# Identity columns in the s products, gate maxima moved by transposes, and five weight granules staged in idle buffers

## The chip, the cores and the metric

The kernel is one program on one core of a Trainium2 chip. The metric is the device time of one execution in microseconds (us). Before the change the median of three runs is 662.71 us (661.94 to 662.95).

## What is computed

A recurrent attention layer (an mLSTM: four batches, eight heads, 768 steps, head size 40) feeds two dense stages on 3072 tokens of 320 numbers:

```python
m_new = max(f_gate[t] + m, i_gate[t])
C = exp(f_gate[t] + m - m_new) * C + exp(i_gate[t] - m_new) * outer(v[t], k[t])
n = exp(f_gate[t] + m - m_new) * n + exp(i_gate[t] - m_new) * k[t]
y[t] = sigmoid(o_gate[t]) * (C @ q[t]) / max(abs(n . q[t]), 1)
x = y.reshape(3072, 320)
h = (x @ w1) * (x @ w2) @ w3 @ w_out          # first stage, d_ff 1024
out = max(x2 @ a1, x2 @ a2, x2 @ a3) @ a_out  # second stage on x2 = h, d_ff 768
```

## The kernel before

**The recurrence in chunks.** Each batch is cut into nine chunks of L = 87 steps (the last has 72), so there are 36 units (`NU`). Unit q = 9b + c is worked on in a visit on TensorE (PE): `visit(v)` computes the s products of unit v (line 839, eight small fp32 products of k and q, one per head) and then the output products of unit v - 1 (line 848). Four heads have their 40 rows at partitions 0 to 39 and four at 64 to 103, and the loop alternates between the two. Each s product loads 87 columns (k) as weights and moves 87 columns (q) past them (72 in the last chunk). An fp32 product stands in the trace as two records, each with its own weight load, so one visit shows sixteen.

The s products are multiplied by decay factors `dd` on VectorE (DVE, line 873) into rows 0 to 86 of a tile `pk`. Rows 87 to 126 of `pk` belong to the state carried over from earlier chunks: there `scaled` (line 806, DVE or GpSimd (POOL)) multiplies q itself, transposed on the host and loaded as the last 696 columns of the tile `kv` (line 706), by `dd`. The output products contract all 127 rows (R = 127) at once. Chunk 0 of each batch has no state, so there is no `scaled` and R is 87. For the first nine units `dd` is made by PE (lines 757 and 758, from `hl`, `one`) and an exponential on ScalarE (ACT, line 761); for the others it is read back from `d_na` in HBM.

**The gates.** At the start, scans on DVE (lines 574 to 612) form the running gate maxima in `gft`. The ones of batch 0 have to come to rows 64 to 72 and 96 to 104 of `hl`: three DMAs write them to `d_na` (line 619), one reads them back (line 650), and ACT and DVE split them in two fp32r parts (lines 651 and 652).

**The weights.** Dense weights arrive as 64-bit numbers in granules of 128 x 512 (512 KB) or 128 x 256, and are turned to fp32 by two ACT or DVE steps (lines 1172, 1178, 1181) and one DVE step (line 1189). Granules rotate through seven buffers at the start: four of the pool `sx`, three of `stg`. `fold(ft)` multiplies w3 by w_out (line 1236, 16 fp32 records for each ft, 128 in all) and leaves it in `wb`; the first two folds run before the first visit, six more between the first visits. From then on the first dense stage (`a_step` and `b_step`, lines 970 to 975, 985 and 1082 to 1086) and the second (`c_step`, `d_step`, lines 970 to 975 and 1102) run, with one visit riding in a dense step now and then.

**Warm-up matmuls.** 22 matmuls of 128 x 512 on zeros (line 541) run at the start: 16 at once, six that wait for the first w_out granule.

**The order.** A planner (`Plan.run`) sorts all operations: each has an engine, a cost in ns, a rank in `PRIO` (lower goes first among those that are ready), and for some a choice of engine in `PICK`. Each engine then runs its operations strictly in the planned order. DMAs are all issued from the queue of SyncE (SP), in order; a DMA whose buffer isn't free holds up those behind it. Tiles share buffers in rotation by tag (`kv` 3, `raw` 2, `raw0` 3, `sx`, `stg`, and in PSUM `wk` 3, `aq` 1).

Of the kernel before, what the change touches and what calls it, by code (L numbers as in the profile page):

```python
# [17 lines left out]
L = 87  # L18
R = L + D
# [32 lines left out]
OC = 4 * L  # L52
BUF = dict(x=3, y=3, ph=2, ev=3, raw=2, kv=3, dd=3, pk=2)
# [12 lines left out]
    "11100111101000000100000110110011111101101111000111010011000110011110110011001110001111001011111110110000110010"  # L66
    "00001011101000111101100110011001101110001010010110011101001010110010111001101100101001110001001000001011111011"
    "10100110000001001110000011011110000100011011010111000100110110100000010000000000100100101000010100111101100110"
    "01000100010000101100001100010011010100110011110001011100000110011001110010111000000"
)  # L70
PRIO = (
# [95 lines left out]
)  # L167
WARM = 11500
USTEPS = (
    (0, 1, 3, 5, 8, 11, 14, 18, 22, 26), (0, 2, 4, 6, 8, 11, 14, 17, 20, 23, 26), (0, 2, 4, 6, 8, 9, 11, 12, 14, 15)  # L170
)
# [1295 lines left out]
```

## Time and profile before

| | us |
|---|---|
| median of three runs | 662.71 (661.94 to 662.95) |
| the profiled execution | 664.29 |
| its span, first to last instruction | 662.6 |
| TensorE busy within it | 648.7 (98%) |
| VectorE, ScalarE, GpSimd busy | 343.7, 296.1, 216.2 |
| HBM read, written | 71.18 MB, 4.03 MB |

The span is what the profile shows; the 1.7 us around it (664.29 less 662.6) aren't in the trace. Busy times of PE are made of records whose ends are modelled and overlap, so the distance between starts tells more of PE's pace than the length of a record. The granted clock of PE is given as a share of 2.4 GHz: 1.00 is that level, 0.50 is 1.2 GHz.

### The profile page before, as it was taken

How to read it: one execution, taken by the hardware profiler on the slowest of the kernel's cores; microseconds unless marked ns; L12 is line 12 of the kernel's file. 1: busy time of each engine (PE TensorE's matmuls, PEld its weight loads, DVE VectorE, ACT ScalarE, POOL GpSimd, SP SyncE). 2: the span in 40 equal slices, each digit the busy share in tenths (PEclk: the TensorE clock that was granted, in tenths of full speed). 3: DMA queues.
4: the chain of work that ended last, by engine and by line, in shares of the span. 5: the costliest groups of instructions: out<-in, count | busy, mean ns of one | idle time of the engine just before them, and what ended most of it. 6: DMA issues, size and time to landing. Idle time of an engine off the chain costs nothing.

```text
span 662.6 us, 14153 instructions
## 1 busy us (share of the span) xinstructions
PE 648.7 (98%) x5903; PEld 574.8 (87%) x5903; DVE 343.7 (52%) x623; ACT 296.1 (45%) x578; POOL 216.2 (33%) x235
## 2 busy tenths in 40 slices
PE   6899999999999999999999999999999999999997
PEld 5676899899999999999999988788788888888897
DVE  5688998877943663554543445464632321322222
ACT  7867986676622363453432343553331122322031
POOL 4052454566413234343244433562300013010030
PEclk9899999999999999999999999999999999999999
DMA  8989973545421453423122343342000010000011
GB/s 288 384 324 368 317 221 125 195 155 171 138 86 56 129 165 124 128 87 95 58 75 85 108 145 119 109 149 65 1 1 1 0 41 1 0 1 0 1 41 40
DMA packets 25489, 76.12 MB, mean 115 GB/s; under 512 B 3145, under 2 KB 6217, under 8 KB 25426
## 3 DMA queue, kind: packets, MB, share of 16 engines
q1 hardware_dynamic: 25426, 75.23, 33.8%
q8 instruction: 46, 0.75, 0.5%
q14 instruction: 17, 0.14, 0.1%
HBM read 71.18 MB, written 4.03 MB: 114 GB/s over the span
## 4 chain that ended last, share of the span: by engine, by line
PE 89%; DMA 3%; DVE 3%; ACT 3%; issue 1%; SPq 0%; ACTq 0%; DVEq 0%
PE wk L970 14%; PE wk L971 13%; PE wk L972 13%; PE wk L973 7%; PE acs L1102 6%; PE wk L975 5%; PE wk L1236 4%; PE aq L848 3%; PE acs L1082 3%; PE acs L1084 3%; PE acs L1086 3%; PE aq L839 3%; PE ac L1102 3%; PE ac L1082 2%; PE ac L1086 2%; PE wk L985 2%
## 5 line engine op out<-in xcount | busy, mean ns | idle before, releaser
L1049 DVE TENSOR_TENSOR misc<-misc,wk 128x384 f32<-128x384 f32 (+2 forms) x87 | 51.3, 594 | 130.5 <-PE wk L975 96.7
L997 ACT CAST hp<-misc 128x384 fp32r<-128x384 f32 (+2 forms) x101 | 55.0, 547 | 141.0 <-DVE misc L1049 53.1
L1001 POOL TENSOR_TENSOR hp<-misc,hp 128x384 fp32r<-128x384 f32 (+1 forms) x40 | 46.2, 1155 | 118.2 <-ACT hp L997 109.0
L970 PE MATMUL wk<-xx,wch 128*128 128x384 f32 (+1 forms) x216 | 77.3, 358 | 0.4 <-DVE misc L1049 0.4
L971 PE MATMUL wk<-xx,wcl 128*128 128x384 f32 (+1 forms) x216 | 76.5, 354 | 0.0
L972 PE MATMUL wk<-xx,wch 128*128 128x384 f32 (+1 forms) x216 | 76.5, 354 | 0.0
L1019 DVE TENSOR_TENSOR misc<-misc,wk 128x384 f32<-128x384 f32 (+1 forms) x56 | 33.8, 607 | 77.7 <-ACT misc L1017 53.2
L970 PE MATMUL wk<-xx,wah 128*128 128x384 f32 (+1 forms) x192 | 69.7, 363 | 1.1 <-DVE misc L1019 0.8
L971 PE MATMUL wk<-xx,wal 128*128 128x384 f32 (+1 forms) x192 | 68.1, 354 | 0.0
L972 PE MATMUL wk<-xx,wah 128*128 128x384 f32 (+1 forms) x192 | 68.0, 354 | 0.0
L1017 ACT COPY misc<-wk 128x384 f32<-128x384 f32 (+1 forms) x56 | 29.3, 522 | 54.8 <-PE wk L975 27.5
L1102 PE MATMUL acs<-wd,hp 128*128 128x320 f32 x234 | 52.7, 310 | 0.1
L1001 POOL TENSOR_TENSOR xx<-misc,hp 128x512 fp32r<-128x512 f32 (+1 forms) x15 | 18.2, 1215 | 95.5 <-ACT hp L997 91.3
L1046 ACT COPY misc<-wk 128x384 f32<-128x384 f32 (+1 forms) x42 | 22.1, 526 | 60.7 <-PE wk L975 46.2
L970 PEld LDWEIGHTS wk<-xx,wch 128*128 128x128 f32 x216 | 40.6, 188 | 3.7 <-DVE misc L1049 0.7
L972 PEld LDWEIGHTS wk<-xx,wch 128*128 128x128 f32 x216 | 40.5, 188 | 3.0
L971 PEld LDWEIGHTS wk<-xx,wcl 128*128 128x128 f32 x216 | 40.6, 188 | 2.8
L1236 PE MATMUL wk<-wof,w 128*128 128x320 f32 x128 | 38.4, 452 | 3.8 <-DVE wof L1189 2.3
L1102 PEld LDWEIGHTS acs<-wd,hp 128*128 128x128 f32 x234 | 40.0, 188 | 1.4 <-ACT misc L1145 0.3
L970 PEld LDWEIGHTS wk<-xx,wah 128*128 128x128 f32 x192 | 36.1, 188 | 4.6 <-DVE misc L1019 1.1
L972 PEld LDWEIGHTS wk<-xx,wah 128*128 128x128 f32 x192 | 36.1, 188 | 2.7
L973 PE MATMUL wk<-xx,wcr 128*128 128x384 f32 (+1 forms) x108 | 38.2, 354 | 0.0
(206 smaller groups left out, 1525.6 us busy)
## 6 DMA issues: line engine op xcount, KB each, us to landing
kv<-in_kv SPq DMA_DIRECT2D x32, 672.0 KB, 4.3
raw<-in_qk SPq DMA_DIRECT2D x36, 348.0 KB, 4.0
dd<-d_na SPq DMA_DIRECT2D x24, 348.0 KB, 3.8
sx<-in_w3t SPq DMA_DIRECT2D x9, 512.0 KB, 6.5
stg<-in_wc SPq DMA_DIRECT2D x9, 512.0 KB, 3.6
out<-misc SPq DMA_DIRECT2D x24, 160.0 KB, 1.9
stg<-in_w3t SPq DMA_DIRECT2D x6, 512.0 KB, 8.6
sx<-in_wa SPq DMA_DIRECT2D x6, 512.0 KB, 8.4
```

The source lines that it names most:

```text
L970: PE.matmul(p, lhsT=h_[:, kt], rhs=xh[:, kt], start=kt == 0, stop=False)
L971: PE.matmul(p, lhsT=l_[:, kt], rhs=xh[:, kt], start=False, stop=False)
L972: PE.matmul(p, lhsT=h_[:, kt], rhs=xl[:, kt], start=False, stop=False)
L973: PE.matmul(p, lhsT=r_, rhs=xh[:, 2], start=False, stop=False)
L975: PE.matmul(p, lhsT=r_, rhs=xl[:, 2], start=False, stop=True)
L997: P.op("A", act(n), lambda sl=sl: A.copy(out=T("ph", key)[:, sl], in_=T(*src)[:, sl]), r=[src + part], w=[("ph", key) + part])
L1001: e.tensor_tensor(out=T("pl", key)[:, sl], in0=T(*src)[:, sl], in1=T("ph", key)[:, sl].bitcast(F32), op=ALU.subtract)
L1019: P.op("V", dve(n), lambda: V.tensor_tensor(out=T(*sa), in0=T(*sa), in1=T(*ps[1]), op=ALU.mult), r=[ps[1]], w=[sa])
L1049: P.op("V", dve(sl.stop - sl.start), lambda sl=sl: V.tensor_tensor(out=T(*sc)[:, sl], in0=T(*sc)[:, sl], in1=T(*ps)[:, sl], op=ALU.max), r ...
L1082: PE.matmul(a, lhsT=w[:, o:o + 128], rhs=h_, start=st, stop=False)
L1102: PE.matmul(T(f"ac{m}", (k, 1)), lhsT=src[:, m * 128:m * 128 + 128], rhs=w[:, o:o + DM], start=first_, stop=last_,)
L1236: PE.matmul(T(*ps), lhsT=T(*w3)[:, i * 128:i * 128 + 128], rhs=wof[:, gt * 320:gt * 320 + 320], start=gt == 0, stop=gt == 7,)
```

## The change

- `raw` gets 40 identity columns behind k for each head (line 789: 214 columns a head in place of 174), from the host. The s products of chunks 1 to 8 load 127 columns as weights in place of 87, so that q itself comes out in PSUM rows 87 to 126 beside the scores. Line 873 then writes all 127 rows of `pk`, and `scaled` is gone. `kv` loses its 696 columns of q; it is 648 columns wide, or 968 where it brings the output gate (all units but the first five).
- The gate maxima of batch 0 go by PE: three transposes into PSUM, a copy to SBUF (`gt`), eight transposes into PSUM (`rp`), from where lines 651 and 652 read. The four DMAs of lines 619 and 650 are gone. `rp` takes the PSUM buffer `aq`, which the first visit uses next.
- Five early granules get other homes: three of w_out the three `kv` buffers, the two 256-column ones of w3 the two `raw` buffers, which unit 8 is the first to use. They no longer count in the rotation through `sx` and `stg`.
- Warm-up matmuls: 13 at once and 3 that wait for `git`, placed ahead of the new transposes, in place of 16 and 6.
- `PICK` and `PRIO` are new throughout, and the planner's constant for the slow clock (`WARM`) goes from 11500 to 8000. The planner's cost of the s products (775 ns) stays.

```diff
+RW = 4 * (2 * L + D)
 PICK = (
...
 PRIO = (
...
-WARM = 11500
+WARM = 8000
...
-        (big, "kv", BUF["kv"], 648 + 8 * L), (big, "raw", BUF["raw"], 8 * L),
+        (big, "kv", BUF["kv"], 1024), (big, "raw", BUF["raw"], RW),
...
-    for n, dep in ((16, ()), (6, (("wo", 0, 0),))):
+    for n, dep in ((13, ()), (3, (("g", "git"),))):
...
-    for i in range(3):
-        dma(100, lambda i=i: SP.dma_start(
-            out=d_na[0, 3 * i:3 * i + 3].rearrange("c h t -> h c t"), in_=c3(T("g", "gft"))[32 * i:32 * i + 8]
-        ), r=[("g", "gft")], w=[("dna", 0, i)])
+    warm(1)
+    new(("pt", 1), [128, 3, LP], F32, "ac0")
+    new(("rp", 0), [128, 2, 512], F32, "aq")
+
+    def f():
+        for c in range(3):
+            PE.transpose(T("pt", 1)[0:L, c, 0:L], c3(T("g", "gft"))[0:L, c], cs[0:L, 0:L])
+
+    P.op("P", 250, f, cols=200, r=[("g", "gft"), ("cs", 0)], w=[("pt", 1)])
+    P.op(("V", "A"), (dve(216), act(216, True)), (
+        lambda: V.tensor_copy(T("gt", 0)[:, :, 0:72], T("pt", 1)[0:L, :, 0:72]),
...
+    def f():
+        for h in range(8):
+            PE.transpose(T("rp", 0)[0:NCH, h // 4, h % 4 * LE:h % 4 * LE + L],
+                         T("gt", 0).rearrange("p c x -> p (c x)")[:, h:8 * 32 + h + 1:32], cs[0:L, 0:L])
+
+    P.op("P", 500, f, cols=400, r=[("gt", 0), ("cs", 0)], w=[("rp", 0)])
...
-    dma(150, lambda: SP.dma_start(out=raw_v, in_=d_na[0, :, :, 0:L]), r=[("dna", 0)], w=[("rv", 0)])
...
-        m = 648 + 8 * L if c else 648 + DM if b else 648
+        m = 648 + DM if (b, c) >= (0, SIGN) else 648
...
-        dma(950, lambda: SP.dma_start(out=T("raw", q).rearrange("p a b -> p (a b)"), in_=qk[b, c, :, 0:8 * L]), w=[("raw", q)])
+        dma(1165, lambda: SP.dma_start(out=T("raw", q).rearrange("p a b -> p (a b)"), in_=qk[b, c, :, 0:RW]), w=[("raw", q)])
...
-        if c:
-
-            def scaled(e):
-                qq = T("kv", q)[:, 648:648 + 8 * L].rearrange("p (h t) -> p h t", t=L)
-                e.tensor_tensor(out=T("pk", q)[64:R, :, 0:n], in0=qq[64:R, :, 0:n],
-                                in1=T("dd", q)[64:R, :, 0:n], op=ALU.mult)
-
-            P.op(("G", "V"), (1600, dve(8 * n)), (lambda: scaled(G), lambda: scaled(V)), r=[("kv", q, "x"), ("kv", q, "g"), ("dd", q)],
-                 w=[("pk", q, 1)], port=1)
...
-                        PE.matmul(s_of(v)[:L, g, h], lhsT=k[:, L:2 * L], rhs=k[:, 0:n], start=True, stop=True)
+                        PE.matmul(s_of(v)[:ub(v)[3], g, h], lhsT=k[:, L:L + ub(v)[3]], rhs=k[:, 0:n], start=True, stop=True)
...
-                out=by_g(T("pk", v)[:L, :, 0:n]), in0=s_of(v)[:L], in1=by_g(T("dd", v)[:L, :, 0:n]), op=ALU.mult
+                out=by_g(T("pk", v)[:rv, :, 0:n]), in0=s_of(v)[:rv], in1=by_g(T("dd", v)[:rv, :, 0:n]), op=ALU.mult
...
-        ng[0] += 1
-        p = "sx" if not switch and i % (STG + EX) < EX else "stg"
-        key = new((p, i), [128, 512, 2], I32, p)
+        ng[0] += not home
+        p = home or ("sx" if not switch and i % (STG + EX) < EX else "stg")
+        key = new(("gr", len(made)) if home else (p, i), [128, 256 if home == "raw" else 512, 2], I32, p)
...
-                granule(wo1[:, i * 512:i * 512 + 512], (("wo", 0, i), lambda i=i: wof[:, i * 512:i * 512 + 512]))
-            warm(1)
+                granule(wo1[:, i * 512:i * 512 + 512], (("wo", 0, i), lambda i=i: wof[:, i * 512:i * 512 + 512]),
+                        "kv" if i < 3 else None)
...
-                        (w3 + part, lambda w3=w3, o=o, n=n: T(*w3)[:, o:o + n]))
+                        (w3 + part, lambda w3=w3, o=o, n=n: T(*w3)[:, o:o + n]), "raw" if n < 512 else None)
```

## Rows read from the trace of the kernel before

**Rows 1.** The page: busy time by engine, and the chain that ended last.

```profile
PE 648.7 (98%) x5903; PEld 574.8 (87%) x5903; DVE 343.7 (52%) x623; ACT 296.1 (45%) x578; POOL 216.2 (33%) x235
PE 89%; DMA 3%; DVE 3%; ACT 3%; issue 1%; SPq 0%; ACTq 0%; DVEq 0%
```

**Rows 2.** Stretches: length, busy us and count by engine, clock, DMA share, GB/s.

```profile
0.00:12.00 12.00, 8.64 (x31) 6.76 (x31) 6.82 (x18) 8.93 (x15) 4.72 (x21) 1.00 0.83 287
12.00:17.00 5.00, 2.68 (x11) 1.58 (x10) 3.47 (x6) 3.65 (x7) 2.57 (x3) 1.00 0.95 291
17.00:21.00 4.00, 3.75 (x8) 2.50 (x9) 2.96 (x6) 1.82 (x4) 0.00 (x0) 0.58 1.00 397
21.00:26.00 5.00, 5.00 (x28) 3.37 (x28) 2.17 (x5) 4.53 (x8) 0.00 (x0) 1.00 0.99 335
...
55.00:72.00 17.00, 15.87 (x247) 12.12 (x234) 13.96 (x31) 13.65 (x30) 5.41 (x7) 1.00 1.00 377
72.00:200.00 128.00, 126.23 (x1289) 121.05 (x1288) 102.02 (x167) 87.70 (x175) 63.19 (x59) 1.00 0.51 164
200.00:662.00 462.00, 458.76 (x3916) 406.56 (x3914) 188.35 (x348) 155.30 (x303) 129.59 (x137) 1.00 0.21 65
```

**Rows 3.** PE's timeline at the start: start, us, work [idle before it, who ended it].

```profile
11.11 1.15 PE L659 MATMUL ac<-cs,misc 32*127 32x32 f32 x9 [1.29 <-ACT sx L1172]
12.56 2.42 PE L1236 MATMUL wk<-wof,w 128*128 128x320 f32 x8 [0.30 <-DVE w L1189]
17.25 8.42 PE L1236 MATMUL wk<-wof,w 128*128 128x320 f32 x24 [2.27 <-DVE wof L1189]
...
28.67 4.58 PE L1236 MATMUL wk<-wof,w 128*128 128x320 f32 x16 [1.05 <-ACT dd L761]
...
66.24 0.43 PE L757 MATMUL wk<-hl,hl 128*128 128x352 f32 x1 [1.13 <-ACT dd L761]
```

**Rows 4.** Pieces of the chain that ended last: start, us, what.

```profile
8.59 6.06 DMA sx<-in_w3t
...
17.25 4.12 PE wk L1236 x8
...
33.57 2.15 PE wk L1236 x8
```

**Rows 5.** Two riding visits in PE's timeline, with 87 and with 72 moving columns.

```profile
211.56 0.78 PE L839 MATMUL aq<-raw 40*87 40x87 f32 x16
212.27 0.81 PE L848 MATMUL aq<-kv,pk 127*32 127x41 f32 x64
...
230.37 0.77 PE L839 MATMUL aq<-raw 40*87 40x72 f32 x16
```

**Rows 6.** By source line: durations in ns, least, median and most, by form.

```profile
L839 PEld LDWEIGHTS aq<-raw x16: 152/154/154, 211.4 to 212.0; 40*87 40x87 f32 x16
L839 PE MATMUL aq<-raw x16: 235/237/238, 211.6 to 212.1; 40*87 40x87 f32 x16
...
L659 PEld LDWEIGHTS ac<-cs,misc x9: 180/186/186, 11.1 to 12.0; 32*127 32x127 f32 x9
L659 PE MATMUL ac<-cs,misc x9: 262/270/270, 11.1 to 12.0; 32*127 32x32 f32 x9
```

**Rows 7.** The same view for the two multiplications into `pk`.

```profile
L806 DVE TENSOR_TENSOR pk<-kv,dd x18: 757/881/2189, 40.3 to 448.3; 63x696 f32<-63x696 f32 x16, 63x576 f32<-63x576 f32 x2
...
L873 DVE TENSOR_TENSOR pk<-aq,dd x33: 755/878/880, 31.5 to 471.4; 87x696 f32<-87x696 f32 x29, 87x576 f32<-87x576 f32 x4
```

**Rows 8.** DVE's timeline around the first products and the gate maxima.

```profile
7.88 0.68 DVE L1189 SCALAR_TENSOR_TENSOR wof<-sx 128x512 int32<-128x512 int32 x1
...
24.79 0.88 DVE L652 TENSOR_TENSOR hl<-misc,hl 9x696 fp32r<-9x696 f32 x1 [0.87 <-ACT hl L651]
```

**Rows 9.** What SP waited for (us, times, longest), and DMA issues, 0 to 80 us.

```profile
SPq L650 <- DMA d_na<-misc: 2.8, 2, 2.6
...
kv<-in_kv SPq DMA_DIRECT2D x8, 672.0 KB, 8.1
```

More of the change, by code (lines that the diff above doesn't have):

```diff
@@ L65 @@
 PICK = (
[L66 to L69, printed above, removed]
+    "10110101111111000000111011101101010110000111100001110000100110101010010111111101111111111001000011110010110000"
+    "10101001101111110111001110110100100110001100010010000100001110010010000001011010010100110011011001111011001111"
+    "01001010000000011011110000110001000010111001100110111011110110101000110011110001001011010001101100101011111101"
+    "1010011001100110110010010000100101110111010010110000"
 )
 PRIO = (
[95 rows of a table removed]
[93 rows of a table added]
 )
-WARM = 11500
+WARM = 8000
 USTEPS = (
@@ L414, in mlstm_moe_kernel @@
         *((big, t, BUF[t], 8 * L) for t in ("dd",)), (big, "pk", BUF["pk"], 8 * R),
-        (big, "kv", BUF["kv"], 648 + 8 * L), (big, "raw", BUF["raw"], 8 * L),
-        (early, "sx", 3, 1024), (tmp, "sx", EX - 3, 1024), (tmp, "w3", L_BUFS, 512), (tmp, "raw0", RAW0, 8 * L),
+        (big, "kv", BUF["kv"], 1024), (big, "raw", BUF["raw"], RW),
+        (early, "sx", 3, 1024), (tmp, "sx", EX - 3, 1024), (tmp, "w3", L_BUFS, 512), (tmp, "raw0", RAW0, RW),
         (psum, "wk", 3, 512), (psum, "aq", 1, 1024),
@@ L524, in mlstm_moe_kernel @@
         o += n
-    made["rv", 0] = misc[:, o:o + 8 * L]
+    made["gt", 0] = misc[0:L, o:o + 3 * LP].rearrange("p (c x) -> p c x", x=LP)
     for tag, (x, y) in where.items():
-        if x < o + 8 * L and o < y:
-            over[tag].append(("rv", 0))
+        if x < o + 3 * LP and o < y:
+            over[tag].append(("gt", 0))
     def c3(t):
@@ L553, in f @@
         pick(cs[:, L:L + 1], cs[:, L:L + 1], -1, L - 1, [[0, 1]], ALU.is_ge, 1.0)
-        e = cs[:, L + 1:L + 1 + NCH]
+        e = cs[:, L + 1:L + 1 + NCH].rearrange("p (i c) -> p i c", c=3)
         for o in (64, 96):
-            pick(e, e, 1, -o, [[-1, NCH]], ALU.not_equal, -1.0)
+            pick(e, e, 1, -o, [[-1, 3], [-3, 3]], ALU.not_equal, -1.0)
     P.op("G", 1200, f, w=[("cs", 0)])
@@ L617, in mlstm_moe_kernel @@
     ), r=[("mp", 0, 0), ("mp", 0, 1)], w=[("g", "aug", 0)])
-    for i in range(3):
-        dma(100, lambda i=i: SP.dma_start(
-            out=d_na[0, 3 * i:3 * i + 3].rearrange("c h t -> h c t"), in_=c3(T("g", "gft"))[32 * i:32 * i + 8]
-        ), r=[("g", "gft")], w=[("dna", 0, i)])
+    warm(1)
[7 more added lines that the diff above has]
+        lambda: V.tensor_copy(T("gt", 0)[:, :, 0:72], T("pt", 1)[0:L, :, 0:72]),
+        lambda: A.copy(out=T("gt", 0)[:, :, 0:72], in_=T("pt", 1)[0:L, :, 0:72]),
+    ), r=[("pt", 1)], w=[("gt", 0)])
+    def f():
[3 more added lines that the diff above has]
+    P.op("P", 500, f, cols=400, r=[("gt", 0), ("cs", 0)], w=[("rp", 0)])
     P.op("G", 400, lambda: G.memset(T("hl", 1)[64:128].bitcast(F32), 0.0), w=[("hl", 1, 2), ("hl", 1, 3)])
@@ L648, in mlstm_moe_kernel, with by4 @@
     P.op("V", dve(NCH * 128), f, r=[("g", "aug"), ("hl", 0, 0)], w=[("hl", 0, 1)])
-    hi, raw_v = T("hl", 1)[64:64 + NCH, :, 0:L], T("rv", 0)[64:64 + NCH].rearrange("p (a b) -> p a b", b=L)
-    dma(150, lambda: SP.dma_start(out=raw_v, in_=d_na[0, :, :, 0:L]), r=[("dna", 0)], w=[("rv", 0)])
-    P.op("A", act(8 * L), lambda: A.copy(out=hi, in_=raw_v), r=[("rv", 0)], w=[("hl", 1, 2)])
-    P.op("V", dve(8 * L), lambda: V.tensor_tensor(
-        out=T("hl", 1)[96:96 + NCH, :, 0:L], in0=raw_v, in1=hi.bitcast(F32), op=ALU.subtract
-    ), r=[("rv", 0), ("hl", 1, 2)], w=[("hl", 1, 3)])
+    def by4(o):
+        return T("hl", 1)[o:o + NCH, :, 0:L].rearrange("p (g h) t -> p g h t", g=2)
+    raw_v = T("rp", 0)[0:NCH, :, 0:4 * LE].rearrange("p g (h t) -> p g h t", t=LE)[:, :, :, 0:L]
+    P.op("A", act(8 * L, True), lambda: A.copy(out=by4(64), in_=raw_v), r=[("rp", 0)], w=[("hl", 1, 2)])
+    P.op("V", dve(8 * L), lambda: V.tensor_tensor(out=by4(96), in0=raw_v, in1=by4(64).bitcast(F32), op=ALU.subtract),
+         r=[("rp", 0), ("hl", 1, 2)], w=[("hl", 1, 3)])
     new(("pt", 0), [128, NCH, 32], F32, "ac2")
@@ L663, in mlstm_moe_kernel @@
     sig = []
-    dma(1700, lambda: SP.dma_start(out=sg0.rearrange("p c d -> p (c d)"), in_=og),
+    dma(2050, lambda: SP.dma_start(out=sg0.rearrange("p c d -> p (c d)"), in_=og),
         w=[("sg", (0, c)) for c in range(SIGN)])
@@ L703, in load @@
         b, c, n, r = ub(q)
-        new(("kv", q), [128, 648 + 8 * L], F32, "kv")
-        m = 648 + 8 * L if c else 648 + DM if b else 648
-        dma(1.36 * m, lambda: SP.dma_start(out=T("kv", q)[:, 0:m], in_=kv[b, c, :, 0:m]), w=[("kv", q, x) for x in "kgx"])
+        new(("kv", q), [128, 648 + DM], F32, "kv")
+        m = 648 + DM if (b, c) >= (0, SIGN) else 648
+        dma(1.36 * m, lambda: SP.dma_start(out=T("kv", q)[:, 0:m], in_=kv[b, c, :, 0:m]), w=[("kv", q, x) for x in "kg"])
     def gates(b, c):
@@ L787, in prepare @@
         b, c, n, r = ub(q)
-        new(("raw", q), [128, 4, 2 * L], F32, "raw0" if q < NQ else "raw")
-        dma(950, lambda: SP.dma_start(out=T("raw", q).rearrange("p a b -> p (a b)"), in_=qk[b, c, :, 0:8 * L]), w=[("raw", q)])
+        new(("raw", q), [128, 4, 2 * L + D], F32, "raw0" if q < NQ else "raw")
+        dma(1165, lambda: SP.dma_start(out=T("raw", q).rearrange("p a b -> p (a b)"), in_=qk[b, c, :, 0:RW]), w=[("raw", q)])
         if (b, c) >= (0, SIGN):
@@ L871, in visit @@
         if v < NU:
-            n = GL[v % NCH]
+            n, rv = ub(v)[2:]
             P.op("V", dve(8 * n), lambda: V.tensor_tensor(
-                out=by_g(T("pk", v)[:L, :, 0:n]), in0=s_of(v)[:L], in1=by_g(T("dd", v)[:L, :, 0:n]), op=ALU.mult
+                out=by_g(T("pk", v)[:rv, :, 0:n]), in0=s_of(v)[:rv], in1=by_g(T("dd", v)[:rv, :, 0:n]), op=ALU.mult
             ), r=[*(t + ("s",) for t in toks), ("dd", v)], w=[("pk", v, 1)])
@@ L1152, in mlstm_moe_kernel, with granule @@
     ng = [0]
-    def granule(src, dst=None):
+    def granule(src, dst=None, home=None):
         n = src.shape[1]
         i = ng[0]
-        ng[0] += 1
-        p = "sx" if not switch and i % (STG + EX) < EX else "stg"
-        key = new((p, i), [128, 512, 2], I32, p)
+        ng[0] += not home
+        p = home or ("sx" if not switch and i % (STG + EX) < EX else "stg")
+        key = new(("gr", len(made)) if home else (p, i), [128, 256 if home == "raw" else 512, 2], I32, p)
         def tl():
@@ L1403, in _lay @@
     qk = pad(qk).reshape(B, 2, D, 2, 4, NCH, L).transpose(0, 5, 1, 2, 4, 3, 6)
-    rows = np.zeros((B, NCH, 128, 704), f)
-    rows[:, :, 0:D, 0:8 * L] = qk.reshape(B, NCH, 2, D, 8 * L)[:, :, 0]
-    rows[:, :, 64:64 + D, 0:8 * L] = qk.reshape(B, NCH, 2, D, 8 * L)[:, :, 1]
-    kvw = np.zeros((B, NCH, 128, 648 + 8 * L), f)
-    kvw[:, :, L:R, 648:] = qk[:, :, :, :, :, 0].transpose(0, 1, 3, 2, 4, 5).reshape(B, NCH, D, 8 * L)
+    one = np.broadcast_to(np.eye(D, dtype=f)[:, None], (B, NCH, 2, D, 4, D))
+    qk = np.concatenate([qk.reshape(B, NCH, 2, D, 4, 2 * L), one], -1).reshape(B, NCH, 2, D, RW)
+    rows = np.zeros((B, NCH, 128, 864), f)
+    rows[:, :, 0:D, 0:RW] = qk[:, :, 0]
+    rows[:, :, 64:64 + D, 0:RW] = qk[:, :, 1]
+    kvw = np.zeros((B, NCH, 128, 648 + DM), f)
     kvt = np.zeros((B, NCH, 128, H, 81), f)
```

188 rows, old and new, of the table PRIO are left out of this document.

## Prediction

> **What bounds the kernel now.** I read the page first: TensorE (PE) is busy for 648.7 of the span's 662.6 us, and 89% of the chain that ended last is PE [rows 1]. Then the table of stretches, to see where that holds [rows 2]. From 72 to 200 us PE is idle for 128.00 - 126.23 = 1.77 us, from 200 to 662 us for 462.00 - 458.76 = 3.24 us, in which the last evacuation lies too. From 72 us on the time is therefore the sum of PE's work, and DVE, POOL and DMA (busy shares in the same rows) have room. A microsecond more of work on PE there is a microsecond more of time; a microsecond less on another engine is nothing. Before 72 us it is different: PE has holes, ACT is busy for 8.93 + 3.65 + 1.82 + 4.53 = 18.9 of the first 26 us, and the DMA share is 0.83 to 1.00 [rows 2]. So the change has to be priced twice: in PE's work from 72 us on, and in the holes before.
>
> **The s products, on PE.** This is the term with the largest price. One visit's sixteen records run from 211.56 to 212.34 us (0.78 us); less the last record's own 0.237 us that is 0.543 us from first start to last start [rows 5, 6]. The two halves of the array (partitions 0 to 39, and 64 up) work side by side, so these are 8 pairs and 7 steps: 0.0776 us a step. What sets the step? With 72 moving columns in place of 87 the sixteen records take 0.77 us, not a sixth less [rows 5]. It isn't the moving columns, then; what both visits have in common is 87 weight columns. A second row shows the same from the other side: the nine transposes at 11.11 us move only 32 columns but load 127, and their step is (1.15 - 0.270) / 8 = 0.110 us at the full clock [rows 2, 3, 6]. 0.110 / 0.0776 = 1.42, and 127 / 87 = 1.46. The loads themselves take 154 ns for 87 columns and 186 ns for 127 [rows 6]: 32 ns more, as the steps do. So with the 40 identity columns I expect a step of 0.110 us: 0.0324 us more, 8 steps a visit, 0.26 us. Chunks 1 to 8 of four batches are 32 visits: 32 x 0.26 = +8.3 us. The low end is 7 steps in the 27 visits after the first folds, 27 x 7 x 0.0324 = +6.1 us, if the first load hides behind the matmul ahead of it and the five early visits fall into holes; the high end is +8.7 us, a load of 186 ns also ending later at the first step of each visit. I take +8.2. The output products read the same `pk` and keep their cost.
>
> The Trainium skill (TensorE: Matmul & The Clock Gate, Step-by-step: what each phase is for) says that throughput is purely N cycles, N being the moving columns. By that the extra weight columns would cost nothing. The trace doesn't bear it out for these small products: 0.77 against 0.78 us.
>
> **What leaves DVE, POOL and SP.** `scaled` goes: 18 instructions of 0.88 us on DVE and 14 on POOL [rows 7]. Line 873 now writes 127 rows, but its time is that of 696 elements a row, 878 ns on 87 rows just as line 806 takes 881 on 63 [rows 7], so it costs the same. This lies beside PE: from 72 us on PE idles 1.77 us up to 200 us for all reasons together [rows 2]. I take 0, bounds -1 and +1. The DMAs shrink: `kv` from 672 to 324 KB for chunks 1 to 4 of batch 0 and to 484 KB elsewhere, `raw` from 348 to 428 KB. Of the eight wide `kv` loads issued in the first 80 us [rows 9] that is about 2.1 MB less, of ten `raw` loads 0.8 MB more. At 340 GB/s the difference is some 4 us of DMA time, but it is worth something only where PE waits for data.
>
> **The start.** Four pieces are lost by PE once it has work: a hole of 2.27 us at 17.25; the eight products after it at the half clock (granted 0.58 on average in that stretch, hence 1.2 GHz for most of it), 4.12 us where eight take 2.15 later, 1.97 lost; a hole of 1.05 us at 28.67 and one of 1.13 us at 66.24 [rows 2 to 4]. Sum 6.4 us. The first hole ends with a w3 granule whose DMA was issued only at 8.59 us, because its `sx` buffer was being read by line 1189 until 7.88 + 0.68 = 8.56 us, and landed 6.06 us later [rows 4, 8]. With five granules in other buffers that DMA can be issued right behind the first ones; the 2.7 MB ahead of it (four granules of 512 KB, two of 256, the gates) at the 350 or so GB/s of these stretches would then have it in SBUF near 11 or 12 us instead of 14.65. The wait of SP for the `d_na` round trip (2.6 us, with w3 granules queued behind it) goes too [rows 9], and `hl`, which was ready only at 25.67 us, can be ready before 17. What is late next is ACT, 18.9 of 26 us busy: the same conversions have to fit in less. So I take the first hole and the half clock as gained (4.2 us) and of the two later holes, which wait for an exponential on ACT, about a third (0.8): -5.0 us. Bounds: 0, if PE still starts its dense run at 17.25; and -8.6, namely all 6.4 and 2.2 us more by doing the first eight products (2.42 us) ahead of 12.56 [rows 3].
>
> **What is added to PE and to the queues.** Eleven transposes at no more than the 0.110 us above are 1.2 us; they and the three later warm-up matmuls can lie in PE's idle time before 12.56 (1.29 us before the nine transposes) [rows 3]: between 0 and +1.2, I take +0.5. PE is strictly in order, so whatever stands behind them waits for `gft`, that is for the gate scans. The first s products now wait for lines 651 and 652, which read `rp` in the buffer `aq`; at some 0.9 us each [rows 8] behind the transposes they end well ahead of 20 us, so nothing. The homes in `kv` and `raw` cost nothing: w_out is out of them before the first `kv` load is wanted, and `raw` isn't used until unit 8.
>
> **The sum** is 8.2 - 5.0 + 0.5 = +3.7 us on the profiled execution's 664.29, 668.0. That execution stands 1.6 us above the median of 662.71, so for the median I give 666.4 us.
>
> **Rivals.** (A) The longer loads are hidden: the step stays at 0.0776 because the load of one half runs behind the matmul of the other. Then only the start counts: -5.0 + 0.5 = -4.5, 658.2 us. The equal times at 72 and 87 moving columns and the 0.110 us of the transposes speak against it; that those transposes all use the same rows of the array and the s products alternate speaks for it. The Trainium skill's rule of the moving columns would come out here. Chance 0.10.
> (B) The start gains enough to pay for the loads. The place is PE's holes in the first 30 us (and the one at 66.24), and it decides from a gain of 8.7 us on: all four pieces and the first products moved ahead of 12.56, practically the bound above. Then 8.2 - 8.6 + 0.5, about 662.8 us, not slower. For it: the w3 data can be there some 3 us sooner. Against: ACT's 18.9 busy us. Chance 0.12.
> (C) The change doesn't do at the start what it says: PE waits at 17.25 for something else (ACT, or the clock falls to 1.2 GHz after the shorter warm-up and the products run at half pace again): 8.2 + 0.5 = +8.7, 671.4 us. For it: DMA was at 0.83 to 1.00 before already [rows 2], so issuing earlier only queues more. Chance 0.10.
> My forecast, a gain of 2.5 to 7 us against the loads' 6.1 to 8.7, has 0.68.
>
> **How the numbers follow.** A difference of 0.2% (1.3 us) is about what a measurement of this kernel tells from none: faster is below 661.4, slower above 664.0. Faster: A with 0.10 and a fifth of B, 0.12. Same: the rest of B and the edge of the forecast, where a gain of 7 meets cheap loads, 0.14. Slower: 0.74. The range from 661.6 to 670.0 holds the forecast's bounds and most of B, and leaves out A and C, about 0.19.
>
> **What will show it.** In the changed kernel, sixteen s records of chunks 1 to 8 should span 7 x 0.110 + 0.237 = 1.01 us in place of 0.78, their loads 186 ns, and from their start to the first output product 0.97 us in place of 0.71 [rows 5]; in chunk 0 nothing changes. PE's busy time from 72 us to the end should grow by about 7 us. The first dense matmul of line 970, the w3 granules' landing and the clock around 12 to 20 us tell of the start; ACT's busy share there tells whether it is late next. I am wrong if the sixteen records still take 0.78 us, or if the first visit starts over 8 us earlier than 25.6.

## Result and the profile after

| | before | after |
|---|---|---|
| median, us | 662.83 (661.94 to 664.74, 4 runs) | 670.22 (668.46 to 670.40, 4 runs) |
| ratio | | 1.0102 [1.0074, 1.0129] |
| profiled execution, its span | 664.29, 662.6 | 670.2, 667.9 |
| first dense matmul starts (line 970, after: 977) | 71.34 | 71.46 |
| from there to the end of the span | 591.3 | 596.4 |

The changed kernel is 7.4 us slower. The last two rows say where: the start gives nothing, and all of the loss in the two profiled spans but 0.1 us lies behind 71 us. The spans differ by 5.3 us only. The profiled execution before stood 1.5 us above its median, and the time outside the span, which no trace shows, is 1.7 us in it and 2.3 to 2.5 us in the four executions after. First the page of the changed kernel, busy time by engine and the chain that ended last:

```profile
PE 656.2 (98%) x5908; PEld 583.1 (87%) x5908; DVE 329.8 (49%) x622; ACT 295.5 (44%) x581; POOL 166.8 (25%) x202
...
PE 92%; ACT 4%; DMA 2%; DVE 1%; issue 1%; POOL 0%; ACTq 0%; DVEq 0%; SPq 0%; POOLq 0%
```

PE is busy for 7.5 us more than in [rows 1], with five matmuls more; DVE and POOL are busy for 63 us less between them, and it bought nothing. Next PE's timeline at two visits of chunks 1 to 8 (87 and 72 moving columns) and at one of chunk 0, which still loads 87 columns (start, us, work); the s products are now line 846, the output products 855:

```profile
207.50 0.44 PE L992 MATMUL wk<-xx,wcr 64*128 64x384 f32 x2
207.78 1.01 PE L846 MATMUL aq<-raw 40*127 40x87 f32 x16
208.72 0.81 PE L855 MATMUL aq<-kv,pk 127*32 127x41 f32 x64
...
229.75 1.00 PE L846 MATMUL aq<-raw 40*127 40x72 f32 x16
230.68 0.81 PE L855 MATMUL aq<-kv,pk 127*32 127x41 f32 x64
...
239.98 0.78 PE L846 MATMUL aq<-raw 40*87 40x87 f32 x16
240.69 0.79 PE L855 MATMUL aq<-kv,pk 127*32 127x41 f32 x48
```

From the first s product to the first output product it is 208.72 - 207.78 = 0.94 us with 127 weight columns and 240.69 - 239.98 = 0.71 with 87, in one kernel, 32 us apart; before it was 212.27 - 211.56 = 0.71 [rows 5]. So a visit costs 0.23 us more, and 72 moving columns save nothing again (0.93). The first eight visits with 127 columns, up to 81 us, cost 0.27 us more (34.08 - 33.03 = 1.05 us for 0.78 before). The durations by form of the s products (least, median and most, in ns):

```profile
L846 PEld LDWEIGHTS aq<-raw x80: 152/187/188, 207.6 to 251.9; 40*127 40x127 f32 x64, 40*87 40x87 f32 x16
L846 PE MATMUL aq<-raw x80: 223/271/271, 207.8 to 252.0; 40*127 40x87 f32 x48, 40*127 40x72 f32 x16, 40*87 40x87 f32 x16
```

A load takes 187 ns in place of 154 [rows 6]. Now the start: the stretches (length, busy us and count by PE, PEld, DVE, ACT, POOL, then granted clock, DMA share, GB/s):

```profile
12.00:17.00 5.00, 3.19 (x7) 1.77 (x8) 3.89 (x6) 4.97 (x10) 0.00 (x0) 0.64 1.01 412
17.00:21.00 4.00, 4.00 (x10) 2.57 (x9) 1.72 (x3) 1.59 (x3) 0.00 (x0) 0.59 1.01 414
...
55.00:72.00 17.00, 17.00 (x297) 13.48 (x296) 13.62 (x30) 16.05 (x35) 9.00 (x10) 1.00 0.93 344
72.00:200.00 128.00, 126.82 (x1286) 122.88 (x1285) 90.19 (x160) 85.93 (x172) 51.93 (x56) 1.00 0.46 150
200.00:667.90 467.90, 463.90 (x3919) 411.52 (x3917) 188.96 (x359) 154.44 (x300) 96.44 (x110) 1.00 0.19 61
```

and PE's timeline there, with the idle time before a piece of work and what ended it:

```profile
10.52 0.78 PE L633 MATMUL aq<-cs,misc 87*9 87x87 f32 x8 [0.89 <-ACT misc L628]
12.01 0.81 PE L1243 MATMUL wk<-wof,w 128*128 128x320 f32 x2 [0.72 <-DVE w L1196]
13.15 0.46 PE L773 MATMUL wk<-hl,hl 128*128 128x352 f32 x1 [0.34 <-DVE hl L669]
...
15.37 8.59 PE L1243 MATMUL wk<-wof,w 128*128 128x320 f32 x22 [1.46 <-DVE wof L1196]
...
26.37 0.85 PE L846 MATMUL aq<-raw 40*87 40x87 f32 x16
27.88 4.57 PE L1243 MATMUL wk<-wof,w 128*128 128x320 f32 x16 [0.65 <-ACT dd L777]
```

Before, there were three holes ahead of the long run of products (1.29, 0.30, 2.27, together 3.86 us) [rows 3]; now there are four (0.89, 0.72, 0.34, 1.46, together 3.41 us). The long run of products starts 1.9 us earlier, but 22 of them take 8.59 us where 24 took 8.42: the granted clock is 0.64 from 12 us on, where before it was 1.00 up to 17 and 0.58 after [rows 2]. The first visit starts at 26.37; before, at 25.59. Behind the same 32 records of folds the next fold starts at 27.88, 0.8 us ahead of before (28.67), and at the first dense matmul that is used up. The data isn't late: SP issues the w3 granules early, while before the first that had to wait for a buffer was issued at 8.59 us,

```profile
3.15 0.50 SPq L1174 DMA_DIRECT2D sx<-in_w3t  x1
...
5.75 0.43 SPq L1174 DMA_DIRECT2D sx<-in_w3t  x1
7.33 1.15 SPq L1174 DMA_DIRECT2D stg<-in_w3t  x2
```

and the DMA moves 412 GB/s from 12 to 17 us against 291. It is the conversions. ACT is busy 4.97 of those 5.00 us, and in the chain that ended last the only transfer up to 30 us is that of the gates, at the very start. These are pieces of the chain:

```profile
0.81 2.71 DMA misc<-in_gi
...
13.44 0.56 ACT sx L1179
14.02 0.03 DVE w L1196
...
14.63 0.69 DVE wof L1196
```

Then PE starts at 15.37. Before, the chain ran through the transfer of a w3 granule, 8.59 to 14.65 us [rows 4]; now ACT and DVE stand there.

### The profile page after: what moved, and what is told of

Same layout as the page of the kernel before. It is cut to its first block, busy times and chain, and to the rows that moved or that the text cites. A ratio compares the mean times of both kernels' runs of the same rounds, so it can differ in the third digit from the quotient of the medians.

```text
span 667.9 us, 14104 instructions
## 1 busy us (share of the span) xinstructions
PE 656.2 (98%) x5908; PEld 583.1 (87%) x5908; DVE 329.8 (49%) x622; ACT 295.5 (44%) x581; POOL 166.8 (25%) x202
## 4 chain that ended last, share of the span: by engine, by line
PE 92%; ACT 4%; DMA 2%; DVE 1%; issue 1%; POOL 0%; ACTq 0%; DVEq 0%; SPq 0%; POOLq 0%
PE wk L977 14%; PE wk L978 13%; PE wk L979 13%; PE wk L980 7%; PE acs L1109 5%; PE wk L982 5%; PE wk L1243 5%; PE aq L846 4%; PE aq L855 4%; PE acs L1089 3%; PE acs L1093 3%; PE acs L1091 3%; PE ac L1109 3%; PE wk L931 2%; PE wk L992 2%; PE ac L1093 2%
## 5 line engine op out<-in xcount | busy, mean ns | idle before, releaser
L880 DVE TENSOR_TENSOR pk<-aq,dd 127x696 f32<-127x696 f32 (+2 forms) x33 | 28.5, 865 | 35.9 <-PE aq L855 34.9
L1008 POOL TENSOR_TENSOR xx<-misc,hp 128x512 fp32r<-128x512 f32 (+1 forms) x13 | 16.0, 1228 | 93.4 <-ACT hp L1004 89.5
```

The costliest lines, as they stand in the source:

```text
L1008: e.tensor_tensor(out=T("pl", key)[:, sl], in0=T(*src)[:, sl], in1=T("ph", key)[:, sl].bitcast(F32), op=ALU.subtract)
```

## Experiments

**Theory.** The longer weight loads cost about 0.24 us in each of 32 visits, some 7.5 us, and are the whole loss; the rebuilt start is worth about nothing, because its holes let PE's clock fall earlier. **Rivals.** The loss lies in the new order, homes and waits, or in the `scaled` product that moved into PE's loads; the start's conversions, not the clock, hold it up.

**1. The longer loads alone: `b_127`.** The kernel before, with 127 weight columns for the s products of chunks 1 to 8 (the extra PSUM rows are written and not used); `raw` gets 40 columns wider for it, and nothing else changes:

```diff
+RW = 8 * L + D
-                        k = raw[g * 64:g * 64 + 40, h]
-                        PE.matmul(s_of(v)[:L, g, h], lhsT=k[:, L:2 * L], rhs=k[:, 0:n], ...)
+                        k = raw[g * 64:g * 64 + 40, h * 2 * L:h * 2 * L + 2 * L + D]
+                        PE.matmul(s_of(v)[:ub(v)[3], g, h], lhsT=k[:, L:L + ub(v)[3]], rhs=k[:, 0:n], ...)
```

> The kernel before with one thing changed: the s products of chunks 1 to 8 load 127 columns as weights in place of 87 (the 40 columns after k in the tile are the next head's q or padding, and nobody reads the rows they give); order, staging, transposes and line 806 stay as before, raw is 20 KB a load longer. Theory (the weight columns set the step of the s products, and PE is saturated): from the first s record to the first output product 0.94 us in place of 0.71, 32 visits of 0.23, so +6.2 (the 27 late visits) to +7.4 us, 669.0 to 670.2 us, the whole of the loss that was measured. Rival (the loss comes from the start and the new order, the loads hide): no more than +1.5 us, below 664.4.

672.96 us, ratio 1.0148 [1.0119, 1.0177]. A visit in PE's timeline:

```profile
213.69 1.02 PE L840 MATMUL aq<-raw 40*127 40x87 f32 x16
214.64 0.81 PE L849 MATMUL aq<-kv,pk 127*32 127x41 f32 x64
```

0.95 us, as in the changed kernel. With this edit the kernel before is 10.6 us slower than its neighbours' median of 662.32 (executions of the kernel before in the same set); the visits themselves are some 7.8 of them, 24 of 0.235 and the first eight of 0.27 us. The first dense matmul starts 1.9 us later than before (73.27), of which six early visits are 1.6. Behind it there is something else. The dense matmuls that the edit doesn't touch, with 384 and 512 moving columns, take 3.6 us more in all from start to start, waits left out. In `b_107` below it is 3.6 us again, in `b_warm` 0.0. So this part comes neither from the visits nor from the number of weight columns. `b_127` and `b_107` share the wider `raw` buffer and its longer load; no run has that alone, so its cause stays open.

**2. The change without the longer loads: `a_87`.** It leaves out the carried state (q isn't put into `pk`), so it is a probe and computes something else; a memset at the start fills the rows that nothing writes. All else, the order too, is that of the changed kernel.

```diff
-                        PE.matmul(s_of(v)[:ub(v)[3], g, h], lhsT=k[:, L:L + ub(v)[3]], rhs=k[:, 0:n], ...)
+                        PE.matmul(s_of(v)[:L, g, h], lhsT=k[:, L:2 * L], rhs=k[:, 0:n], ...)
```

> The changed kernel with 87 weight columns in every s product, all else as it is; the rows of the carried state are left out, so the output lacks what earlier chunks carry over (one VectorE memset at the start fills the PSUM rows that nobody writes). It is the start's part of the change alone. Theory (the loads are the whole loss, the start by itself gained next to nothing since the clock ran low for longer): 32 visits of 0.24 us less, 7.5 us below the changed kernel, 661.5 to 663 us, no different from before. Rival (the start gained the 5 us that were forecast, and the new order lost them again in the dense part): under 659 us is impossible then only if the dense part is slower by as much, which its span from the first dense product to the end would show: over 594 us in place of 591.3.

663.44 us (12 runs), ratio 1.0005 [0.9989, 1.0021]. The changed kernel itself, beside it on the same chip (`after_again`), took 669.33 us:

> The changed kernel itself, beside the three others on the same chip, so that what each of them changes is read in one place. Both theories: 668.5 to 670.5 us, +6 to +8 on the kernel before.

Ratio 1.0100 [1.0075, 1.0125], the first result again. So 5.9 us of the changed kernel's 6.3 go with 40 weight columns, and the rest of the change as a whole is worth nothing that can be measured. PE's timeline of `a_87`, a visit and the start:

```profile
15.41 7.76 PE L1247 MATMUL wk<-wof,w 128*128 128x320 f32 x22 [1.29 <-DVE wof L1200]
...
25.58 0.85 PE L850 MATMUL aq<-raw 40*87 40x87 f32 x16
```

```profile
208.22 0.78 PE L850 MATMUL aq<-raw 40*87 40x87 f32 x16
208.93 0.81 PE L859 MATMUL aq<-kv,pk 127*32 127x41 f32 x64
```

Visits of 0.71 us, and a first visit at 25.58 us; before, 25.59.

**3. A size between: `b_107`.** As `b_127`, with 107 columns.

> The kernel before with 107 weight columns in the s products of chunks 1 to 8, halfway between 87 and 127 (the 20 columns more give rows that nobody reads). Theory (a step grows with the weight columns, 0.83 ns a column): loads of 170 ns, from the first s record to the first output product 0.82 to 0.83 us (0.71 with 87, 0.94 with 127). Rival (a step between two fixed values, as of a limit at 96 columns or of the array's last quarter): 0.71 or 0.94 us.

```profile
214.39 0.90 PE L840 MATMUL aq<-raw 40*107 40x87 f32 x16
215.22 0.81 PE L849 MATMUL aq<-kv,pk 127*32 127x41 f32 x64
```

0.83 us, half way between 0.71 and 0.95: the price goes with the weight columns, and there is no step between 87 and 127. Its one time, 671.98 us, is nearly that of `b_127`, though its visits add only 32 x 0.12 = 3.8 us: in its trace 6.6 us are added from the first dense matmul to the last, 3.0 by visits and 3.6 by the other matmuls named above.

**4. The loads cut in two: `a_split` and `a_split2`.** Each s product of the changed kernel as two matmuls, on weight columns up to 64 and from 64 on. `a_split` does it in all chunks, so chunk 0 gets halves of 64 and 23 columns; `a_split2` leaves chunk 0 whole.

```diff
-                            PE.matmul(s_of(v)[:ub(v)[3], g, h], lhsT=k[:, L:L + ub(v)[3]], ...)
+                            for a, e in ((0, 64), (64, R)) if v % NCH else ((0, L),):
+                                PE.matmul(s_of(v)[a:e, g, h], lhsT=k[:, L + a:L + e], ...)
```

> The changed kernel with each s product cut in two by weight columns, 0 to 63 and 64 to the end, which write PSUM rows 0 to 63 and 64 on and so use the left and the right half of the array's columns. The result is the same. Theory (a step is set by the weight columns of one load, 127 x 2 / 2.4 GHz, and loads into different halves of the columns run side by side): the step falls back to what 87 moving columns take, 0.71 us or so to the first output product, and the time by 32 x 0.23 = 7.4 us to 662.8 (661.8 to 664). Rival (the halves load one after the other, or twice the instructions cost what is saved): 669 to 671 us.

687.92 us, ratio 1.0384 [1.0347, 1.0421]: far from every expectation. PE's timeline at a visit of chunk 0, and the stretches around it (columns as above):

```profile
25.77 4.97 PE L847 MATMUL aq<-raw 40*64 40x87 f32 x32
```

```profile
25.00:31.00 6.00, 6.00 (x37) 3.20 (x36) 2.52 (x6) 4.84 (x10) 1.01 (x1) 0.85 1.03 392
31.00:36.00 5.00, 5.00 (x10) 3.20 (x10) 1.93 (x3) 0.00 (x0) 0.00 (x0) 0.50 0.22 88
```

The 32 records of this chunk-0 visit take 4.97 us, 0.155 us each; the granted clock is 1.00 up to 29 us and at 1.2 GHz from 30 us on, before the visit has ended. The four such visits take 4.97, 4.45, 4.92 and 4.45 us where whole ones take 0.78 to 0.85. That is 15.5 of the 18.6 us that `a_split` lies above `after_again`. In all other visits the same cut helped, which `a_split2` shows by itself:

> The changed kernel with the s products of chunks 1 to 8 cut in two by weight columns (0 to 63, 64 to 126), those of chunk 0 left whole. In the first split kernel a visit of chunk 0, whose second part is 23 columns wide, took 4.97 us, and the others 1.13 us from the products ahead of the s products to the output products, against 1.22 in the changed kernel and 0.99 before. Theory (the first split kernel's loss is the four chunk-0 visits and the clock that fell in them): 32 x 0.09 = 2.9 us below the changed kernel, 666 to 668 us. Rival (splitting costs in every visit): as slow as or slower than the changed kernel.

```profile
206.81 0.44 PE L993 MATMUL wk<-xx,wcr 64*128 64x384 f32 x2
207.18 0.83 PE L847 MATMUL aq<-raw 40*64 40x87 f32 x32
207.94 0.81 PE L856 MATMUL aq<-kv,pk 127*32 127x41 f32 x64
```

667.51 us, 1.8 below `after_again`; the six runs of each overlap (665.99 to 670.29 and 668.82 to 671.57). The visit shows it better. From the matmul before the visit to the first output product it is 207.94 - 206.81 = 1.13 us; uncut 208.72 - 207.50 = 1.22. (From the first s product it is 0.76, but the first one starts 0.09 later.) 32 x 0.09 = 2.9 were expected; somewhat less came. What this kernel does with 72 moving columns tells which side sets the pace:

```profile
228.96 0.73 PE L847 MATMUL aq<-raw 40*64 40x72 f32 x32
229.62 0.81 PE L856 MATMUL aq<-kv,pk 127*32 127x41 f32 x64
```

With the loads cut, 72 moving columns take 0.66 us to the first output product and 87 take 0.76. Uncut they take 0.93 and 0.94. So with whole loads the weight side sets the pace, and with cut loads the moving columns count. Whether it is the smaller load or the other half of the array that helps, no run separates.

**5. Is it the clock that eats the start? `a_warm`.** The changed kernel with 12 matmuls on idle data in its first holes: 3 behind the three transposes, 3 behind the eight, 6 behind the first gate-maximum products.

```diff
+    def hum(n):
+        for i in range(n):
+            PE.matmul(acs[:, 512:1024], lhsT=wb[:, NA - 1, 512:640], rhs=wb[:, NA - 1, 0:512], start=True, stop=True)
```

> The changed kernel with twelve more warm-up matmuls on zeros in PE's holes: 3 behind the first three transposes, 3 behind the eight, 6 behind the first pair of lines 773 and 774. Theory (at the start the gain was eaten by the clock: PE ran at 1.2 GHz from 13.4 to 20.2 us, 3.4 us longer than before, because its holes lie between 9.6 and 15.4 us): the clock stays at 1.00, the 22 products from 15.4 us on take about 6 us in place of 8.2, and the time falls by 1.5 to 2.4 us to 667.8 to 668.7. Rival (PE waits for granules, and ACT and DVE are late with them at any clock): holes in place of slow products, less than 0.6 us gained, 669.6 or more.

666.69 us (11 runs), ratio 1.0059 [1.0043, 1.0076], 2.6 below `after_again` and 3.5 below the first result; no run of it is as slow as the fastest of theirs (667.81, 668.46). The granted clock over the whole execution is 0.999 or 1.000 in all 11 runs, and 0.991 to 0.995 in the ten of the changed kernel. The stretch from 12 us, and PE's timeline:

```profile
12.00:17.00 5.00, 4.40 (x17) 2.89 (x17) 3.89 (x6) 4.97 (x10) 0.00 (x0) 1.00 1.03 424
```

```profile
15.39 6.19 PE L1251 MATMUL wk<-wof,w 128*128 128x320 f32 x22 [0.26 <-DVE wof L1204]
...
23.98 0.85 PE L854 MATMUL aq<-raw 40*87 40x87 f32 x16
...
69.49 0.34 PE L985 MATMUL wk<-xx,wah 128*128 128x384 f32 x1
```

The clock stays at 1.00. The run of 22 products starts at the same time as without (15.39 and 15.37), and the same pieces of ACT and DVE stand before it in the chain that ended last, so they hold it there; but it takes 6.19 in place of 8.59 us, and the first dense matmul starts 2.0 us earlier. Both causes are real: the conversions set when the run starts, the clock how long it takes.

**6. Is that worth as much before? `b_warm`, `b_warm2`.** The kernel before with 8 such matmuls behind its first eight products (`b_warm`), and with 5 more in its early warm-up too (`b_warm2`).

> The kernel before with eight warm-up matmuls on zeros in PE's hole of 2.27 us ahead of 17.25. Theory (the loss at the start, in both kernels, is the clock that falls because of the holes): the granted clock stays at 1.00, the products from 17.25 us on take 0.27 us each from the first, 1.7 to 2 us are gained, 660.3 to 660.8 us in these runs. Rival (the products wait for w3 granules at either clock): 662 us or more, with new holes between 17 and 26 us.

662.79 us, ratio 1.0002 [0.9985, 1.0018]: nothing. PE's timeline shows what became of the eight:

```profile
12.12 4.11 PE L1240 MATMUL wk<-wof,w 128*128 128x320 f32 x8 [0.30 <-DVE w L1193]
...
17.91 6.62 PE L1240 MATMUL wk<-wof,w 128*128 128x320 f32 x24
```

In this execution the clock had fallen ahead of the 8 added matmuls: the first eight products took 4.11 us (2.42 in [rows 3]), behind a hole of 1.60 us at 10.68. Even so its first dense matmul starts at 69.20, 2.1 us ahead of the profiled execution before (71.34), and the medians are the same. The profiled execution before is a slow one of its kernel (664.29, median 662.83), so its 71.34 may be late for that kernel, and the start of the changed kernel may look better beside it than it is. With that hole filled too:

> The kernel before with warm-up matmuls in both holes of PE at the start: five more behind the first 22, ahead of the nine transposes, and the eight ahead of 17.25. With the eight alone the clock fell at 12.59, behind the first hole, before they ran. Theory (the holes let the clock fall, and where it falls differs from execution to execution): the clock stays at 1.00 through 12 to 21 us, and the time is 1.5 to 2 us below before, 661 to 661.6 us for 663.0. Rival (granules hold the products up anyway): within 0.7 us of before.

```profile
12.16 2.42 PE L1240 MATMUL wk<-wof,w 128*128 128x320 f32 x8 [0.30 <-DVE w L1193]
...
16.27 6.62 PE L1240 MATMUL wk<-wof,w 128*128 128x320 f32 x24
```

The half clock is gone here (24 products in 6.62 us, 8.42 before), but of the time only 0.9 us: 662.37 us, ratio 0.9988 [0.9970, 1.0005]. It is no measurable gain (the holes of PE move on, 0.36 and 0.72 us by 26.33), and the clock falls once later instead (0.88 from 26 to 40 us). No kernel of this study clearly beats the one before.

**7. Do the two mends add? `a_split2_warm`.**

> The changed kernel with both repairs, the s products of chunks 1 to 8 cut at column 64 and the twelve warm-up matmuls in PE's holes. Theory (the two losses are separate: weight loads in the dense part, the clock at the start): the gains add, about 1.8 from the cut and 2.5 to 3.5 from the clock, 664 to 665 us. Rival (they share a cause): no better than the warm-up matmuls alone, 666 to 667 us.

664.38 us (12 runs), ratio 1.0023 [1.0003, 1.0044]: 5.0 us below `after_again`, where 1.8 and 2.6 are 4.4. Within the noise they add. What is left of the loss is 1.1 us, and some 0.6 of it lies outside the span: 2.0 to 2.5 us in these executions, 1.6 to 1.8 in those of the kernel before. No run shows why.

**8. Two that didn't tell: `a_nohome`, `a_start`.** `a_nohome` takes the five new homes away (`home = None`), `a_start` is `a_warm` with the s products and `scaled` of the kernel before.

> The changed kernel without the homes: the five early granules go through sx and stg in rotation as before the change, order and all else as in the changed kernel. Theory (the homes let SP issue the w3 granules early, and the start holds on to it): w3 DMAs wait for line 1196 again, the first visit comes 1 to 3 us later and the time is 671 to 673 us. Rival (DMA was loaded anyway and ACT or the clock is late next): within 0.7 us of 670.2.

695.36 us, ratio 1.048 [1.044, 1.052]. The stretch from 72 us:

```profile
72.00:200.00 128.00, 115.66 (x1250) 107.32 (x1249) 83.91 (x151) 79.75 (x163) 49.84 (x54) 0.95 0.43 139
```

PE idles for 12.3 us in a stretch where it idled for 1.2. The order was made for granules that come early. That it waits with late ones, and that this is the price of an order that doesn't fit and not that of the homes, is a reading; no run shows it, and what the homes are worth stays open.

> The start of the changed kernel (staging, transposes, ranks) with the twelve warm-up matmuls in PE's holes, and the s products of the kernel before: 87 weight columns, q carried in kv and multiplied by dd on VectorE (two instructions ahead of the output products in place of one, 32 x 0.88 us more of VectorE beside PE). Theory (the loss is the weight loads alone, and the start is worth its 3 us once the clock holds): 32 x 0.24 = 7.6 us below the changed kernel with these warm-up matmuls (666.7), 659 to 661 us, faster than both kernels. Rival (VectorE's 28 us more come between the s products and the output products and PE waits for them, so the identity columns were worth their loads): 664 us or more.

692.62 us, ratio 1.0436 [1.0407, 1.0465]. A stretch, and the longest of PE's waits from 60 to 100 us (us in total, times, longest):

```profile
72.00:100.00 28.00, 19.80 (x239) 16.93 (x237) 22.53 (x43) 19.14 (x41) 8.15 (x10) 0.88 0.38 131
```

```profile
PE wk L779 <- ACT dd L785: 3.0, 2, 1.9
PE wk L945 <- POOL misc L937: 2.7, 2, 2.5
```

Here `scaled` all goes to DVE (32 instructions, 28.9 us, which the changed kernel doesn't have) without a place in the order, and PE waits for `dd` and for results of the recurrence. The rival's condition, PE waiting behind DVE, isn't separated from an order that doesn't fit, so this run doesn't tell what `scaled` is worth. What the new start would be worth with the old s products, the warm-up matmuls and an order made for them stays open; `a_87` shows only that without these warm-up matmuls nothing came of it, though nothing took DVE's time.

## Why the prediction was right, and where it wasn't

The sum said 668.0 us for the profiled execution, which took 670.2, and 666.4 for the median, which is 670.2; slower, by the reason given. But the loss is 7.4 us where 3.7 were forecast. The measured median lies at the very top of the range of 661.6 to 670.0 (662.71 times the ratio of 1.0102 is 669.5), nearer to rival C's 671.4 than to the forecast. The forecast rested on a gain of 2.5 to 7 us at the start, and that gain didn't come; the loads alone make the changed kernel slower. Its steps:

- **PE sets the time from 72 us on: right.** A visit's 0.23 us comes out in the time, and DVE's and POOL's 63 us less don't: PE idled 1.77 us from 72 to 200 [rows 2], now 1.18. From the first dense matmul to the end it is 5.1 us more; 26 visits lie there, not the 27 of the prediction, and cost 6.2, so the rest of the change gave back 1.1, of which 0.6 are these shorter waits. The term for DVE and POOL (0, bounds 1 either way) holds.
- **The price of the loads: right in mechanism, a twentieth too high.** Forecast 0.110 us a step, 1.01 us for the records, loads of 186 ns; measured (1.01 - 0.271) / 7 = 0.106, 1.01 and 187. The steps plus the later end of the last one were put at 0.26 us a visit and are 0.235 in 24 visits and 0.27 in the first eight: 7.8 in place of 8.2. The transposes of [rows 3, 6], another form on other rows, foretold the pace of the s products. The Trainium skill (TensorE: Matmul & The Clock Gate, Step-by-step: what each phase is for) makes throughput a matter of the moving columns alone; the trace disagrees, since 127 x 87 and 127 x 72 take 1.01 and 1.00 us. The same page (LDWEIGHTS) gives a load as its columns divided by 1.2 in ns; by an estimate from that, 40 more are 33 ns, and the trace agrees (154 to 187), though not on a whole load (for 87 columns the estimate is 73 ns, the trace shows 154).
- **Rival A, hidden loads: fell.** 40 columns more or less make 10.6 us in `b_127` and 5.9 in `a_87`, and the visits themselves 7.8.
- **The start, -5.0 us: this is the term that failed.** Net it gave nothing: the first dense matmul 71.46 for 71.34, with 1.6 us of longer early visits in it; `a_87`, without those, ends within the noise of before. The prediction took the first hole (2.27) and the half clock (1.97) as gained, on the ground that the w3 data would be there. The data was there. But behind that transfer stood ACT, 4.97 of 5.00 us busy, and PE's holes ahead of the long run only went from 3.86 to 3.41 us. That ACT would be late next was in the text and yet not in the number. And the half clock was treated as gone with the hole. It came back with the others: with four holes from 9.6 us on it fell earlier and lasted longer, 22 products in 8.59 us, which `a_warm`, with the holes filled, does in 6.19. Whether the shorter warm-up had a part in it no run separates. That is rival C's mechanism (671.4 us, chance 0.10), and it should have had far more: 7.8 with nothing against them, and the median rose by 7.4.
- **The two later holes: more than counted.** A third of them was counted, 0.8 us. The hole at 66.24 is gone (from 55 to 72 us PE is busy 17.00 of 17.00, 15.87 before [rows 2]), and that of 1.05 us at 28.67 is 0.65 at 27.88: 1.5 us.
- **The transposes, +0.5:** the eight take 0.78 us in a stretch where PE idles anyway. No run takes them out, so what they cost isn't shown.

Why the same 40 columns make 10.6 us in the order of before and 5.9 in the new one is told in part by the traces. The visits differ alike in both. `b_127` has besides them the 3.6 us of other matmuls from above, whose cause is open. In `a_87` the shorter visits leave PE waiting: from 72 to 200 us it idles 2.38 us, 1.18 in the changed kernel, and all other dense matmuls keep their pace within 0.1 us in all. The clock isn't the reason for the 10.6: the execution of `b_127` with a granted clock of 1.000 took 672.54 us, the four of the kernel before beside it with 1.000 took 661.00 to 663.54.

## What to carry to other kernels

A product with few moving columns can cost what its weights cost, as these did with 40 rows and 72 or 87 moving columns: before columns are added to the weights to save work elsewhere, multiply the added load time by the steps on the bounding engine, and set it against what the relieved engine gives back, which is nothing while that engine isn't the one waited for. A hole that ends with a transfer is gained only if everything else in that stretch, here the conversions on ACT and DVE, has room; read the busy share of each engine there before taking the hole as won. And a hole moved is not a clock regained: the sum of PE's idle time alone doesn't tell (3.86 us before, 3.41 after, with the clock low for longer), so read the granted clock behind the holes, and try a few matmuls on idle data in them. That gave 2.6 us back in the changed kernel and nothing measurable in the kernel before.

## What the hardware showed beyond that

- **Uneven halves are dear.** Weight columns cut into 64 and 63 took 0.83 us for 32 records, cut into 64 and 23 they took 4.97. The Trainium skill (TensorEngine Tiling (Array Packing), Key Properties) says that a change of tiling mode, other than one of tile, drains TensorE. That would fit if the 23 columns run in a narrower mode; no run here shows it or tells it from another cause.
- **The clock can fall behind work that counts as busy.** In `a_split` PE is busy 6.00 of 6.00 us from 25 to 31 us, and from 31 to 36 us the granted clock is 0.50: the 32 slow records count as busy in the profile, and yet it fell. It fell at or behind the other three slow visits too (0.57 from 104 to 108 us, 0.59 from 250 to 256, 0.84 from 396 to 402).
- **Where the clock falls isn't fixed.** The changed kernel's second profiled execution has it lower and for longer than the first over the same stretches (0.64 and 0.59 above):

```profile
12.00:17.00 5.00, 3.67 (x7) 2.18 (x8) 3.90 (x6) 4.97 (x10) 0.00 (x0) 0.50 1.02 409
17.00:21.00 4.00, 4.00 (x9) 2.45 (x8) 1.73 (x3) 1.64 (x3) 0.00 (x0) 0.50 1.02 417
```

Filling the holes doesn't always hold the times together: `a_warm` took 666.04 to 667.81 us in 11 runs, `a_split2_warm`, with the same matmuls, 663.61 to 668.69 in 12, the slowest with a granted clock of 0.995.
